# GpSimd tied to VectorE's planned order, no normalisation on GpSimd, re-priced plan and one copy less a pair in an attention and two-expert-layer kernel

## The chip, the cores and the metric

One core of one Trainium2 chip. The time is the device time of one execution in microseconds; the median of three runs counts. The engines are named as in the profile: PE is TensorE (PEld its weight load), DVE is VectorE, ACT is ScalarE, POOL is GpSimd, SP is SyncE, whose queue issues the DMAs.

## The reference

Three layers, all in fp32, for 4 batches of 448 tokens with a model width of 768.

```python
# 1. causal attention: q, k, v are (4, 12, 448, 64)
scores = scale * q @ k.T;  scores = where(above the diagonal, -1e9, scores)
attn = exp(scores - max);  attn = attn / (sum(attn) + 1e-9);  x = attn @ v
# 2. gated convolution layer: w_in (768, 1024), conv_w (3, 1024), w_out (1024, 768)
h = maximum(x @ w_in, 0)
conv = sum over k of conv_w[k] * h shifted by k - 1 tokens
x = (h * sigmoid(conv)) @ w_out
# 3. four experts, each one head of causal attention with its own wq, wk, wv (768, 64) and wo (64, 768)
logits = x @ w_gate;  the two largest of four get softmax weights w
out = sum over experts of w[e] * (attention_e(x) @ wo[e])
```

## The kernel before

Every fp32 operand of a large product is split into a high part and a low part (`high` at L666 copies it rounded, `low` at L677 subtracts the high part), and a product is three matmuls: high x high, low x high, high x low (`products`). The output weights of layer 2 are multiplied once into the projections of layer 3 (`fold`), so the kernel runs, for each batch: attention over 6 pairs of heads, 8 feed-forward parts (`ffn_in`), the projections of the experts (`project`), attention over 2 pairs of experts, and the output product (`output`).

Attention of a pair (`scores`, `norms`, `weigh`): 24 score matmuls into PSUM; DVE adds the mask and takes the extreme (L711); ACT takes the exponential and its sum (L715); each of 10 pieces of the weights `e` is then multiplied by the reciprocal of its sum (`norm` inside `norms`: L760 on ACT, L763 on DVE or GpSimd, of 64, 192, 320 or 384 columns; for experts the gate is multiplied in as well, and then ACT is not allowed); 14 transposes on PE (L781) put the weights into PSUM tiles `ta` and `tb`, 8 copies (L670 on ACT, L672 on DVE) bring them to the SBUF tile `z`, and 16 matmuls (L814) multiply the values. There is one tile `z`. Two of the 8 copies have 512 columns, two 256, and four 128 on 64 partitions. The result is again split into high and low.

No engine's order is written by hand. Each step is an operation of a `Plan` with a price for each engine that may run it (`scale_cost`, `psum_cost`, `copy_cost`, `two_cost`) and lags between engines (`LAG`). The planner runs list scheduling: it picks engine and start of each operation by rank, and the instructions are emitted in order of planned start. The ranks come from backward passes and are then changed by a long list of adjustments, `SHIFTS`; a list entry adds a constant or a noise of a seed to the ranks of some operations. On the chip each engine runs its instructions in the order emitted, and waits only for what it reads and overwrites. In the plan, operations that use the SBUF port shared by DVE and GpSimd (every GpSimd operation, and those of DVE whose `port` has a "V") exclude one another; the emitted program does not hold to that.

Six dummy matmuls (`WARM`) and thirty more (`FILLS`) run on PE ahead of the first data.

Of the kernel before, what the change touches and what calls it, by code (L numbers as in the profile page):

```python
# [17 lines left out]
B, H, S, D = 4, 12, 448, 64  # L18
# [25 lines left out]
KEYS = ((0, 448), (448, 320), (832, 192), (768, 64))  # L44


def spread(z, width, first, step, n):
# [168 lines left out]
class Plan:  # L216
# [4 lines left out]
    LAG = {"TT": 0.0, "TA": 0.2, "TV": 0.2, "TG": 0.27, "TD": 0.19, "AT": 0.23, "AA": 0.0, "AV": 0.16, "AG": 0.17, "AD": 0.14,  # L221
# [130 lines left out]
    def run(self):  # L352
# [35 lines left out]
        if SHIFTS and forward(rank) >= best[0]:  # L388
            forward(best[1])
        for o in sorted(self.ops, key=lambda o: (o.start, o.n)):  # L390
            o.fn(o.engine)

# [149 lines left out]

ON = {"qk high": ("AVG", "AVG"), "qk low": "VG", "gx": "AG", "w high": "AVG", "w low": "VG"}
# [16 lines left out]
def scale_cost(n, on="AVG"):  # L560
    return only(on, {"A": on_scalar(n) + 0.137, "V": on_vector2(n) + 0.065, "G": 0.245 + n * 0.000835})
# [6 lines left out]
def psum_cost(n, on="A"):  # L568
    return dict(only(on, {"A": on_scalar(n), "V": on_vector(n)}))
# [5 lines left out]


@with_exitstack
def attention_moe_moe(ctx: ExitStack, tc: tile.TileContext, qk, vv, w_in, cw, w_out, wqk, wvg, wo, out):
    nc = tc.nc
    ctx.enter_context(tc.manual_schedule())  # L580
    P = Plan()

    w1d = nc.dram_tensor("w1_scratch", (NF, 128, 2 * DM), F32, kind="Internal").ap()
    wod = nc.dram_tensor("wo_scratch", (2, 128, 2 * DM), F32, kind="Internal").ap()

    base = ctx.enter_context(tc.tile_pool(name="base", bufs=1))
    psum = ctx.enter_context(tc.tile_pool(name="psum", bufs=1, space=PSUM))
# [629 lines left out]
```

## Time and profile before

| what | value |
|---|---|
| median of three runs | 534.32 us (533.75 to 536.55) |
| the profiled execution | 535.11 us, span of its instructions 533.3 us |
| granted TensorE clock, mean over the span | 0.992 of full speed |
| busy: PE, DVE, ACT, POOL | 515.4, 421.6, 357.7, 112.0 us |
| DMA | 69.92 MB, 131 GB/s over the span |

The span runs from the first instruction to the end of the last one, and the execution's own time is 1.8 us longer. Busy time of PE counts a matmul from its issue to a modelled end, so matmuls that queue behind each other are counted as busy as well. Times in the trace are from the span's start.

### The profile page before, as it was taken

To read this page: it belongs to the slowest core of one execution; us is meant where nothing else is said; L and a number is where in the kernel's file an instruction comes from. 1 tells how busy PE (TensorE), PEld (TensorE's weight loads), DVE (VectorE), ACT (ScalarE), POOL (GpSimd) and SP (SyncE) were. 2 spreads that over 40 slices of the span, in tenths; PEclk is the share of its full clock that TensorE was granted. 3 is DMA by queue.
4 is the path that set the end of the run, shared out by engine and by line. 5 is a ranking of instruction groups with operands and counts; after the bars stand their busy time and mean duration, and the time that the engine had idled before them with its cause. 6 is when DMAs were issued, how large, how long until landed. Compare 5 with 4: busy or idle time off the path is not lost.

```text
span 533.3 us, 10436 instructions
## 1 busy us (share of the span) xinstructions
PE 515.4 (97%) x3554; PEld 436.2 (82%) x3556; DVE 421.6 (79%) x1300; ACT 357.7 (67%) x1058; POOL 112.0 (21%) x132
## 2 busy tenths in 40 slices
PE   8799999899899999899999999999999999999997
PEld 4678888778689898798898777998987778989875
DVE  6999599889798549999259999986389999842581
ACT  2876279789986557686249986755488867732572
POOL 3152017334232021160012511101114000000010
PEclk9999999899989999999999999999999999999999
DMA  9984246845587011374201573763003315610042
GB/s 239 256 222 135 63 149 195 255 120 206 167 246 201 23 36 37 139 250 163 68 2 46 146 219 84 249 215 87 1 1 113 117 49 194 221 59 1 10 154 104
DMA packets 63381, 69.92 MB, mean 131 GB/s; under 512 B 36576, under 2 KB 57312, under 8 KB 63328
## 3 DMA queue, kind: packets, MB, share of 16 engines
q1 hardware_dynamic: 63328, 69.26, 42.7%
q8 instruction: 28, 0.46, 0.4%
q14 instruction: 25, 0.20, 0.1%
HBM read 55.87 MB, written 13.37 MB: 130 GB/s over the span
## 4 chain that ended last, share of the span: by engine, by line
PE 47%; DVE 25%; ACT 8%; issue 2%; ACTq 0%; DVEq 0%
PE pf L966 34%; DVE e L711 7%; DVE e L763 5%; PE bank L814 5%; DVE z L672 4%; PE bank L781 3%; ACT e L715 3%; PE bank L734 3%; ACT e L760 2%; DVE pair L678 1%; DVE pair L672 1%; DVE work L995 1%; PE bank L966 1%; ACT z L670 1%; PE pf L1074 1%
## 5 line engine op out<-in xcount | busy, mean ns | idle before, releaser
L966 PE MATMUL pf<-pair,slab 128*128 128x448 f32 (+2 forms) x984 | 218.5, 368 | 4.3 <-ACT hp L984 2.7
L966 PEld LDWEIGHTS pf<-pair,slab 128*128 128x128 f32 x984 | 171.8, 189 | 22.2 <-ACT hp L984 3.7
L715 ACT ACTIVATE e<-e,stat 128x192 f32<-128x192 f32 (+3 forms) x256 | 127.1, 499 | 23.8 <-DVE stat L711 23.4
L711 DVE CUSTOM_DVE_ANT_0 e<-bank,mask 128x448 f32<-128x448 f32 (+3 forms) x256 | 92.1, 414 | 6.7 <-PE bank L734 6.5
L966 PE MATMUL pf<-pair,wqks 128*128 128x448 f32 x384 | 81.1, 369 | 0.0
L966 PEld LDWEIGHTS pf<-pair,wqks 128*128 128x128 f32 x384 | 71.4, 188 | 7.0 <-ACT pair L670 0.3
L781 PE MATMUL bank<-ident,e 128*128 128x128 f32 x448 | 70.7, 280 | 6.4 <-DVE stat L711 3.5
L678 POOL TENSOR_TENSOR pair<-work,pair 128x448 fp32r<-128x448 f32 (+1 forms) x39 | 48.6, 1260 | 105.6 <-PE bank L734 39.1
L781 PEld LDWEIGHTS bank<-ident,e 128*128 128x128 f32 x448 | 52.7, 142 | 16.9 <-DVE stat L711 3.6
L672 DVE COPY z<-bank 64x128 f32<-64x128 f32 (+2 forms) x121 | 48.7, 429 | 20.9 <-PE bank L781 16.7
L670 ACT ACTIVATE z<-bank 64x128 f32<-64x128 f32 (+2 forms) x135 | 45.8, 367 | 13.4 <-PE bank L814 7.4
L760 ACT ACTIVATE e<-e,stat 64x64 f32<-64x64 f32 (+3 forms) x116 | 49.4, 454 | 7.5 <-DVE stat L755 5.9
L734 PE MATMUL bank<-pair,pair 64*128 64x448 f32 (+3 forms) x576 | 49.6, 291 | 0.1
L814 PE MATMUL bank<-z,block 128*64 128x448 f32 (+3 forms) x384 | 48.7, 395 | 0.0
L715 ACT ACTIVATION_READ_ACCUMULATOR e<-e,stat 128x1 f32 (+1 forms) x256 | 48.5, 189 | 0.0
L995 DVE SCALAR_TENSOR_TENSOR work<-hp,cws,work 128x448 f32<-128x448 f32 x64 | 43.7, 694 | 3.9 <-ACT work L990 3.3
L734 PEld LDWEIGHTS bank<-pair,pair 64*128 64x128 f32 (+1 forms) x576 | 41.9, 172 | 3.3 <-issue 1.6
L814 PEld LDWEIGHTS bank<-z,block 128*64 128x64 f32 x384 | 27.3, 139 | 20.6 <-issue 11.5
L966 PE MATMUL pf<-wvs,pair 128*128 128x260 f32 x288 | 37.3, 286 | 0.0
L678 DVE TENSOR_TENSOR pair<-pf,pair 64x448 fp32r<-64x448 f32 (+1 forms) x24 | 15.0, 623 | 26.7 <-ACT pair L670 26.4
L966 PEld LDWEIGHTS pf<-wvs,pair 128*128 128x128 f32 x288 | 35.5, 188 | 0.3
L670 ACT ACTIVATE pair<-pf 64x448 fp32r<-64x448 f32 (+1 forms) x24 | 12.8, 541 | 32.3 <-PE pf L966 32.0
(99 smaller groups left out, 593.7 us busy)
## 6 DMA issues: line engine op xcount, KB each, us to landing
slab<-w_scratch SPq DMA_DIRECT2D x24, 768.0 KB, 4.6
work<-in_w_out SPq DMA_DIRECT2D x8, 768.0 KB, 4.8
work<-in_w_in SPq DMA_DIRECT2D x8, 768.0 KB, 5.7
w_scratch<-slab SPq DMA_DIRECT2D x8, 768.0 KB, 4.5
work<-in_qk SPq DMA_DIRECT2D x48, 112.0 KB, 3.4
work<-in_qk SPq DMA_DIRECT2D x24, 224.0 KB, 4.3
out<-work SPq DMA_DIRECT2D x24, 224.0 KB, 2.1
slab<-wo_scratch SPq DMA_DIRECT2D x6, 768.0 KB, 4.3
```

The source lines that it names most:

```text
L670: nc.scalar.activation(dst(), src(), AF.Copy)
L672: nc.vector.tensor_copy(dst(), src())
L678: return lambda e: engine(e).tensor_sub(dst(), src(), f32(h()))
L711: nc.vector.tensor_tensor_reduce(out=ec(o, c), in0=bank(o, c), in1=m, scale=-0.125, scalar=3.0e38, op0=OP.add, op1=OP.min, accum_out=st[ro ...
L715: nc.scalar.activation(ec(o, c), ec(o, c), AF.Exp, bias=st[rows, 0, o, c:c + 1], scale=-1.0, accum_out=st[rows, 1, o, c:c + 1])
L734: nc.tensor.matmul(bank(o, c), q(s)[own, Q0[c]:Q0[c] + QN[c]], k(t)[own, kc(o, c)], start=i == 0, stop=i == 2)
L760: nc.scalar.activation(dst(), src(), AF.Copy, scale=st[rows, 3, o, c:c + 1])
L763: engine(en).tensor_scalar(dst(), src(), st[rows, 3, o, c:c + 1], gate, op0=OP.mult, op1=OP.mult)
L781: P.op({"T": TURN}, lambda _: nc.tensor.transpose(dst(), src(), ident[:, :]), r=r, w=keys)
L814: nc.tensor.matmul(ps[own, S - n:S], v(k, o), z[:, 1024 * o + n0:1024 * o + n0 + n], start=k == 0, stop=k == 3)
L966: nc.tensor.matmul(out_ap(), a(), b(), start=first, stop=end), r=r, w=[(ps, 0)])
L995: return lambda _: nc.vector.scalar_tensor_tensor(cv[:, :S], hp[:, i:S + i], cws[:, fc, i:i + 1], cv[:, :S], op0=OP.mult, op1=OP.add)
```

## The change

- `LAG["AA"]`, between dependent ACT operations, goes from 0.0 to 0.15. `scale_cost` becomes dearer by 0.053 (ACT), 0.05 (DVE) and 0.055 (GpSimd), `psum_cost` by 0.12 below 64 columns and by 0.065 up to 128. The convolution's first step keeps its old price.
- `norm` may run on ACT or DVE (attention) or DVE only (experts); GpSimd is no longer allowed.
- On emission, the first instruction of each GpSimd operation gets a dependency on the last instruction of the port-using DVE operation emitted just before it, if that one was planned to start less than 3 us earlier.
- The columns of `z` are laid out anew (`KEYS`), so that what was copied from `ta` in two copies of 256 columns is copied in one of 512.
- The last output tile is copied and stored in two halves.
- `SHIFTS` is a new list.

```diff
-KEYS = ((0, 448), (448, 320), (832, 192), (768, 64))
+KEYS = ((0, 448), (704, 320), (512, 192), (448, 64))
...
-    LAG = {"TT": 0.0, "TA": 0.2, "TV": 0.2, "TG": 0.27, "TD": 0.19, "AT": 0.23, "AA": 0.0, "AV": 0.16, "AG": 0.17, "AD": 0.14,
+    LAG = {"TT": 0.0, "TA": 0.2, "TV": 0.2, "TG": 0.27, "TD": 0.19, "AT": 0.23, "AA": 0.15, "AV": 0.16, "AG": 0.17, "AD": 0.14,
...
+        body, near = self.nc.cur_bb.bb, None
         for o in sorted(self.ops, key=lambda o: (o.start, o.n)):
+            n = len(body.instructions)
             o.fn(o.engine)
+            new = body.instructions[n:]
+            if o.engine == "V" and "V" in o.port:
+                near = o, new[-1].name
+            elif o.engine == "G" and near and near[0].start > o.start - 3:
+                self.tc.add_manual_dep(new[0], near[1], mybir.DependencyInfo(mybir.DependencyClass.Sync, mybir.DependencyReason.DATA), reason="port")
...
+NORM = ("AV", "V")
...
-    return only(on, {"A": on_scalar(n) + 0.137, "V": on_vector2(n) + 0.065, "G": 0.245 + n * 0.000835})
+    return only(on, {"A": on_scalar(n) + 0.19, "V": on_vector2(n) + 0.115, "G": 0.3 + n * 0.000835})
...
-    return dict(only(on, {"A": on_scalar(n), "V": on_vector(n)}))
+    more = 0.12 if n < 64 else 0.065 if n <= 128 else 0.0
+    return dict(only(on, {"A": on_scalar(n) + more, "V": on_vector(n) + more}))
...
-            P.op(scale_cost(n, "VG" if moe else "AVG"), fn, r=r + [(st, "r")] + ([(COEF, b)] if moe else []), w=w)
+            P.op(scale_cost(n, NORM[moe]), fn, r=r + [(st, "r")] + ([(COEF, b)] if moe else []), w=w)
...
-            for o in range(2):
-                P.op(psum_cost(256, "AV"), high(lambda o=o: spread(z, 2048, 1024 * o + 64, 832, 128),
-                                                lambda t=t, o=o: t[:, 256 * o:256 * o + 256].rearrange("p (b c) -> p b c", b=2)),
-                     r=[(t, 2 * o), (t, 2 * o + 1)], w=[(z, (o, 3))])
+            P.op(psum_cost(512, "AV"), high(lambda: z[:, :].rearrange("p (a b) -> p a b", a=4)[:, :, 64:192],
+                                            lambda t=t: t[:, :].rearrange("p (a b) -> p a b", a=4)), r=[(t, j) for j in range(4)], w=[(z, 3)])
...
-            P.op(scale_cost(S, "A"), c1, r=[(hp, 0), (CWS, 0)], w=[(cv, 0)])
+            P.op({"A": on_scalar(S) + 0.137}, c1, r=[(hp, 0), (CWS, 0)], w=[(cv, 0)])
...
-            P.op(psum_cost(S, "AV"), high(lambda o=o: o[:, :S], lambda ps=ps: ps[:, :S]), r=[(ps, 0)], w=[(o, 0)])
+            parts = 1 + (b + 1 == B and dc + 1 == NK)
+            for i in range(parts):
+                own = slice(i * S // parts, (i + 1) * S // parts)
+                P.op(psum_cost(S // parts, "AV"), high(lambda o=o, own=own: o[:, own], lambda ps=ps, own=own: ps[:, own]), r=[(ps, 0)], w=[(o, i)])
+                P.op(dma_cost(229376 // parts, 1792 // parts), lambda _, dc=dc, o=o, own=own: nc.sync.dma_start(out[b, dc][:, own], o[:, own]), r=[(o, i)])
```

## Rows read from the trace of the kernel before

**Rows 1.** The page's part 1: busy time, share of the span, instructions.

```profile
PE 515.4 (97%) x3554; PEld 436.2 (82%) x3556; DVE 421.6 (79%) x1300; ACT 357.7 (67%) x1058; POOL 112.0 (21%) x132
```

**Rows 2.** The chain that ended last: start, length in us, what.

```profile
153.64 1.70 PE bank L734 x24
...
184.46 1.88 PE bank L814 x16
...
335.69 22.49 PE pf L966 x111
...
388.39 1.31 PE bank L781 x12
...
529.86 0.55 ACT work L670
```

**Rows 3.** By stretch: length, busy of PE, PEld, DVE, ACT, POOL, clock, DMA share, GB/s.

```profile
80.00:145.00 65.00, 60.64 (x433) 50.60 (x429) 57.91 (x161) 58.55 (x173) 29.62 (x31) 0.97 0.63 191
195.00:240.00 45.00, 43.62 (x313) 37.49 (x312) 43.16 (x150) 33.78 (x105) 12.06 (x12) 1.00 0.39 126
275.00:321.00 46.00, 44.85 (x388) 36.08 (x382) 44.16 (x178) 41.83 (x137) 16.44 (x22) 1.00 0.43 121
...
400.00:440.00 40.00, 38.72 (x325) 29.72 (x324) 39.00 (x151) 32.08 (x109) 8.20 (x13) 1.00 0.28 93
```

**Rows 4.** The page's part 4: that chain's shares of the span by engine.

```profile
PE 47%; DVE 25%; ACT 8%; issue 2%; ACTq 0%; DVEq 0%
```

**Rows 5.** L763 alone, whole span: busy of DVE, POOL, clock, DMA share, GB/s.

```profile
0.00:533.30 533.30, 54.22 (x151) 31.19 (x53) 0.99 0.43 131
```

**Rows 6.** L763 on GpSimd: count, duration in ns (least/median/most), first and last start, shapes.

```profile
L763 POOL TENSOR_SCALAR e<-e,stat x42: 313/538/1123, 18.7 to 428.3; 64x64 f32<-64x64 f32 x15, 128x384 f32<-128x384 f32 x12, 128x320 f32<-128x320 f32 x9, 128x192 f32<-128x192 f32 x6
...
L763 POOL TENSOR_SCALAR e<-e,stat,coef x11: 390/606/4227, 211.8 to 511.2; 64x64 f32<-64x64 f32 x4, 128x320 f32<-128x320 f32 x3, 128x192 f32<-128x192 f32 x2, 128x384 f32<-128x384 f32 x2
```

**Rows 7.** DVE by shape in 440:459: busy us, mean ns, idle before.

```profile
L678 DVE TENSOR_TENSOR pair<-work,pair 128x448 fp32r<-128x448 f32 x4 | 2.4, 622 | 0.1
...
L763 DVE TENSOR_SCALAR e<-e,stat,coef 64x64 f32<-64x64 f32 x4 | 1.2, 310 | 0.1
...
L763 DVE TENSOR_SCALAR e<-e,stat,coef 128x384 f32<-128x384 f32 x2 | 0.9, 478 | 0.0
L763 DVE TENSOR_SCALAR e<-e,stat,coef 128x320 f32<-128x320 f32 x2 | 0.8, 434 | 0.0
...
L763 DVE TENSOR_SCALAR e<-e,stat,coef 128x192 f32<-128x192 f32 x2 | 0.7, 379 | 0.0
```

**Rows 8.** ACT by shape, whole span.

```profile
L670 ACT ACTIVATE z<-bank 128x512 f32<-128x512 f32 x30 | 17.3, 588 | 2.2 <-PE bank L781 1.9
...
L760 ACT ACTIVATE e<-e,stat 64x64 f32<-64x64 f32 x48 | 15.9, 344 | 1.0
L760 ACT ACTIVATE e<-e,stat 128x384 f32<-128x384 f32 x21 | 12.8, 609 | 0.1
...
L670 ACT ACTIVATE z<-bank 128x256 f32<-128x256 f32 x34 | 11.7, 379 | 2.6 <-PE bank L781 2.3
```

**Rows 9.** DVE by shape, whole span.

```profile
L678 DVE TENSOR_TENSOR pair<-work,pair 128x448 fp32r<-128x448 f32 x45 | 29.1, 652 | 1.6 <-ACT pair L670 1.2
L672 DVE COPY z<-bank 128x512 f32<-128x512 f32 x34 | 22.8, 683 | 10.1 <-PE bank L781 6.4 <-PE bank L814 3.3
...
L672 DVE COPY z<-bank 128x256 f32<-128x256 f32 x30 | 11.4, 413 | 5.5 <-PE bank L781 5.5
```

**Rows 10.** The timeline around 391.2 us: start, length, engine, instruction.

```profile
391.19 1.16 POOL L678 TENSOR_TENSOR pair<-work,pair 128x448 fp32r<-128x448 f32 x1
391.26 1.28 DVE L763 TENSOR_SCALAR e<-e,stat 128x320 f32<-128x320 f32 x1
```

**Rows 11.** Waits of DVE and of PE: total us, times, longest.

```profile
DVE pair L678 <- ACT pair L670: 31.6, 17, 4.8
...
PE pf L966 <- POOL pair L678: 0.4, 1, 0.4
```

More of the change, by code (lines that the diff above doesn't have):

```diff
@@ L581, in attention_moe_moe @@
     P = Plan()
+    P.tc, P.nc = tc, nc
     w1d = nc.dram_tensor("w1_scratch", (NF, 128, 2 * DM), F32, kind="Internal").ap()
@@ L791, in weigh @@
         for o, own in enumerate(HALF):
-            P.op(psum_cost(128, "AV"), high(lambda own=own, o=o: spread(z, 2048, 1024 * o, 448, 64)[own],
+            P.op(psum_cost(128, "AV"), high(lambda own=own, o=o: spread(z, 2048, 1024 * o, 704, 64)[own],
                                             lambda own=own, t=t: t[own, :128].rearrange("p (b c) -> p b c", b=2)), r=[(t, 1)], w=[(z, (o, 0))])
-            P.op(psum_cost(128, "AV"), high(lambda own=own, o=o: z[own, 1024 * o + 768:1024 * o + 896], lambda own=own, t=t: t[own, 128:256]),
+            P.op(psum_cost(128, "AV"), high(lambda own=own, o=o: z[own, 1024 * o + 448:1024 * o + 576], lambda own=own, t=t: t[own, 128:256]),
                  r=[(t, 2)], w=[(z, (o, 1))])
@@ L802, in weigh @@
             if i < 2:
-                P.op(psum_cost(512, "AV"), high(lambda i=i: spread(z, 2048, 1024 * i + 192, 320, 256), lambda t=t: t[:, :].rearrange("p (b c) -> p b c", b=2)),
+                P.op(psum_cost(512, "AV"), high(lambda i=i: spread(z, 2048, 1024 * i + 192, 576, 256), lambda t=t: t[:, :].rearrange("p (b c) -> p b c", b=2)),
                      r=[(t, j) for j in range(4)], w=[(z, (i, 2))])
                 continue
-            for o in range(2):
-                P.op(psum_cost(256, "AV"), high(lambda o=o: spread(z, 2048, 1024 * o + 64, 832, 128),
-                                                lambda t=t, o=o: t[:, 256 * o:256 * o + 256].rearrange("p (b c) -> p b c", b=2)),
-                     r=[(t, 2 * o), (t, 2 * o + 1)], w=[(z, (o, 3))])
+            P.op(psum_cost(512, "AV"), high(lambda: z[:, :].rearrange("p (a b) -> p a b", a=4)[:, :, 64:192],
+                                            lambda t=t: t[:, :].rearrange("p (a b) -> p a b", a=4)), r=[(t, j) for j in range(4)], w=[(z, 3)])
         def rest(_):
@@ L814, in rest @@
                     nc.tensor.matmul(ps[own, S - n:S], v(k, o), z[:, 1024 * o + n0:1024 * o + n0 + n], start=k == 0, stop=k == 3)
-        P.op({"T": 4 * 960 / 2400 + 0.23}, rest, r=[(z, (o, i)) for o in range(2) for i in range(4)] + v_r, w=[(ps, 0)], mode=2)
+        P.op({"T": 4 * 960 / 2400 + 0.23}, rest, r=[(z, (o, i)) for o in range(2) for i in range(3)] + [(z, 3)] + v_r, w=[(ps, 0)], mode=2)
         P.op(psum_cost(S, "AV"), high(lambda: dst[:, 0], lambda: ps[:, :S]), r=[(ps, 0)], w=[(dst, 0)])
@@ L1153, in output @@
                  [(hi, 0)], [(lo, 0)], [(ys[p], 0)], [(ys[p], 1)]) for p in range(2)])
-            P.op(psum_cost(S, "AV"), high(lambda o=o: o[:, :S], lambda ps=ps: ps[:, :S]), r=[(ps, 0)], w=[(o, 0)])
-            P.op(dma_cost(229376, 1792), lambda _, dc=dc, o=o: nc.sync.dma_start(out[b, dc], o[:, :S]), r=[(o, 0)])
+            parts = 1 + (b + 1 == B and dc + 1 == NK)
[3 more added lines that the diff above has]
+                P.op(dma_cost(229376 // parts, 1792 // parts), lambda _, dc=dc, o=o, own=own: nc.sync.dma_start(out[b, dc][:, own], o[:, own]), r=[(o, i)])
     xs = attention(0)
```

120 rows, old and new, of the table SHIFTS are left out of this document.

## The prediction, made before the change was run

> **What bounds the kernel now.** I read the busy times of the engines first [rows 1]. TensorE is marked busy for 515.4 of 533.3 us, but a matmul that waits in the pipeline counts as busy, so I price its work by itself. Stretches of the chain of waits in which TensorE runs without a stop [rows 2] give: 22.49 us for 111 matmuls of 448 columns, 0.2026 us each; 1.31 us for 12 transposes, 0.109 us; 1.70 us for the 24 score matmuls of a pair of heads; 1.88 us for its 16 value matmuls. From the loops of the code there are 1104 products of 448 columns, 144 of 512, 496 of 260, 496 transposes and 32 pairs. With the other widths priced by columns the work is 1104 x 0.2026 + 144 x 0.2316 + 496 x 0.1176 + 496 x 0.109 + 32 x 3.58 = 223.7 + 33.3 + 58.3 + 54.1 + 114.6 = 484 us. So 49 us of the span are not TensorE work. The tail behind the last matmul takes 3.4 (the last ACT copy begins at 529.86), the 36 dummy matmuls ahead of the first data some 8 (36 x 0.2316). About 37 us are left, lost in the middle.
>
> The table of busy time by stretch says where [rows 3]. In 195:240, 275:321 and 400:440 VectorE (DVE) is busy 43.16 of 45, 44.16 of 46 and 39.00 of 40 us: these stretches, with 80:145 where ACT is as full as DVE, carry most of the attention work. Over the whole span DVE is busy only 79% [rows 1], so elsewhere it has room while TensorE runs dense. The summary of the chain [rows 4] agrees: a quarter of the span hangs on DVE work, 8% on ACT. So the time is TensorE's work plus what the crowded DVE stretches cost it, and an edit is worth what it takes from DVE there, or what the order moves out of there.
>
> **The change part by part.**
>
> *No normalisation on GpSimd.* 53 instructions leave it, 31.19 us of its time [rows 5]. Their shapes [rows 6]: in the attention stages 15 of 64 columns, 9 of 320, 12 of 384, 6 of 192; in the expert stages (they multiply by a gate) 4, 3, 2, 2. Prices on DVE come from a stretch with hardly any GpSimd work [rows 7]: 0.310, 0.434, 0.478, 0.379. The 11 expert ones can go to DVE only: 4 x 0.310 + 3 x 0.434 + 2 x 0.478 + 2 x 0.379 = 4.3 us. The 42 others would cost DVE 16.6, or ACT 20.2 (0.344 and 0.609 for 64 and 384 columns [rows 8], 0.45 and 0.56 between them for 192 and 320). I take them halved between the engines: DVE +8.3, ACT +10.1. Bounds: DVE +4.3 to +20.9 altogether. ACT has 6.4 + 11.2 + 4.2 + 7.9 = 30 us free in the four crowded stretches [rows 3], which hides its share; without that cover it would cost up to 10.
>
> *One copy less a pair.* The new layout of z lets one 512-column copy replace two of 256. ACT: 2 x 0.379 - 0.588 = 0.170 us saved [rows 8]; DVE: 2 x 0.413 - 0.683 = 0.143 [rows 9]. Over 32 pairs, half on each: DVE -2.3, ACT -2.7. The Trainium skill (Perfetto Trace Analysis, "Optimizing Scalar/DVE Operations") puts the fixed part of a PSUM access at about 125 ns on DVE and 51 ns on ACT; by it the saving is an estimated -2.0 and -0.8, so the trace is kinder to ACT, and DVE's term would move by 0.3 us. The other side: the copy now waits for all four transposes, and the last one to land takes 0.59 to 0.68 instead of 0.38 to 0.41, so z is whole 0.21 to 0.27 us later for each pair, 6.7 to 8.6 us over 32 if bare. I cost it at nothing: between the transposes and the value matmuls TensorE has products of the feed-forward part to run, and in crowded stretches DVE's total counts, not one pair's latency.
>
> *GpSimd waits for the DVE instruction planned just ahead of it.* What it is to cure is in one pair of rows [rows 10]: a GpSimd subtraction of 1.16 us starts 0.07 us before a DVE normalisation of 320 columns, and that takes 1.28 us instead of 0.434: it ends when GpSimd ends. The sum of this is less than the one case looks. The 45 DVE subtractions between SBUF tiles average 0.652 [rows 9] against 0.622 undisturbed [rows 7]: 0.03 each, 1.35 us. With some 290 such instructions (the 45 subtractions, 151 normalisations [rows 5], 64 and up to 32 of the convolution) at that rate it is 8.8 us. Between 1.35 and 8.8 I take 6, as longer single cases exist; two thirds go away: DVE -4. Bounds: 0 to -8.8. For the cost of the wait: behind a waiting GpSimd instruction stand the next low halves of its queue, and for these waits TensorE. It waited for GpSimd's halves once in the whole profile, 0.4 us [rows 11], and GpSimd's 112.0 us [rows 1] fall by 31, so I cost the wait at nothing; were each of the 79 remaining GpSimd instructions late by one DVE instruction (0.62 us), 49 us of GpSimd idleness would still fit in its 533.
>
> *Freed GpSimd time.* 31.19 us hold 26 subtractions of 1.16 us. Each taken from DVE saves 0.622. The planner chooses the engine; I count half, 13: DVE -8.1 (bounds 0 and -16).
>
> *Split last output.* The last copy of 448 columns (0.55 us on ACT [rows 2]) becomes two of 224, one on each engine, each with its own store. Half of the copy goes: -0.3 us. Bounds: 0 (the second store is queued behind the first on SP) to -0.55.
>
> *Measured prices and new order.* The planner's price of an ACT normalisation of 384 columns was 0.05 + 0.32 + 0.137 = 0.507 against 0.609 in the row; now it is 0.56. For 64 columns it was 0.240 against 0.344. For an ACT instruction that feeds another it now adds 0.15. So plan and execution drift apart less, and with engines that run in order, drift is what makes one late instruction hold up everything behind it. The ranks that set the order are a wholly new list. What this is worth no row shows. Above: the 37 us lost in the middle. Below: an order can open a new wait, and the longest of the DVE waits for ACT's high half was 4.8 us [rows 11]: +4.8. Most of the DVE work stays and TensorE stays near its 484, so I stay far from the upper end: a fifth, -7.
>
> *Sum.* DVE in the crowded stretches: +4.3 + 8.3 - 2.3 - 4 - 8.1 = -1.8. Last output -0.3, order -7: -9.1. On the profiled execution's 535.1 that is 526.0; this execution lies 0.8 above the median of 534.3, so 525.2.
>
> **Rivals.**
>
> *A larger gain from the order.* If half of the 37 us comes back, as the higher GpSimd share and the closer prices allow: -18 - 2 = -20, 514. For it: DVE is idle for 21% of the span [rows 1] while it is full in the crowded stretches [rows 3]. Against: the batches depend on each other, so attention can be moved only so far.
>
> *No change.* DVE ends even (the planner moves no subtractions: +6.3) and the order gives back just that: 533, anywhere in 531.6 to 537.0, which is 0.5%, about what a measurement of this kernel can tell from no change.
>
> *Slower: the collisions change sides.* The added wait is one-sided: GpSimd waits for DVE, DVE never for GpSimd. A GpSimd instruction now starts just when the DVE one ahead of it ends, which is when DVE begins its next; if that one also works between SBUF tiles, DVE stands for the whole of it, as in [rows 10]. The place is the crowded stretches. Price: 35 subtractions there now (48 for queries and keys and 32 for the gate values, less DVE's 45) plus 13 more, 48, each holding DVE for half of 1.16 us in half of the cases (the other half read PSUM) is 48 x 0.58 x 0.5 = +14; without the -4 and without an order gain DVE has +2.2 + 14, 550; with half of these prices 542. It decides when more than a third of the GpSimd instructions are followed on DVE by an instruction between SBUF tiles. For it: nothing on DVE's side waits. Against: the planner itself keeps such instructions apart, and DVE has PSUM readers to put beside them. The Trainium skill (SBUF — State Buffer, "Who interferes with whom") states this as a rule: whoever of the two issues first has the shared pair for its whole instruction and the other blocks. By that rule the trace agrees in the 1.28 us row, and by it the wait alone moves a stall and does not remove it.
>
> **How the numbers follow.** Forecast case, 519 to 531.6: 0.50. Larger gain, below 519: 0.17. No change: 0.19. Slower: 0.14. Faster is 0.50 + 0.17 = 0.67. The time is that of the likeliest, 525.2. The range takes the larger gain down to 512 and the no-change case up to 537 and leaves out the slower one and a little below: 512 to 537. The forecast case alone is 519 to 531.6.
>
> **What would show it.** Right: no normalisation left on GpSimd; mean time of DVE subtractions between SBUF tiles near 0.62 and of the cast and normalisation forms near their undisturbed values; 32 more 512-column copies and no 256-column ones; more than 35 subtractions on GpSimd; less DVE-bound chain than a quarter of the span; the last matmul some 9 us earlier. Wrong: GpSimd rows that end DVE's idle or stretch its instructions more than now, TensorE waiting for GpSimd's low halves, or DVE full over longer stretches than the four. The prediction fails most easily in the size of the order's term, which is a choice within wide bounds.

## The result and the profile after

The changed kernel takes 522.04 us (median of 4 runs, 521.72 to 522.63) against 534.15 (median of 4): ratio 0.9758, 95% interval 0.9732 to 0.9784, 12.1 us faster. The prediction was 525.2, within 512 to 537. The profiled execution took 521.82 us, its span 520.0.

The page of the changed kernel, parts 1 and 4, answers [rows 1] and [rows 4]:

```profile
PE 510.4 (98%) x3556; PEld 434.5 (84%) x3556; DVE 416.7 (80%) x1313; ACT 357.4 (69%) x1062; POOL 79.3 (15%) x86
...
PE 86%; DVE 8%; ACT 3%; DMA 1%; issue 1%; SPq 0%; ACTq 0%
```

GpSimd's work falls by 32.7 us and DVE's falls too, by 4.9, although DVE now does more normalisations. The chain that ended last runs through DVE for 8% of the span where it was 25%. It is one path through a crowd of near-equal ones, so this is a sign and not a sum of time.

By stretch (the columns are those of [rows 3]):

```profile
80.00:150.00 70.00, 69.87 (x523) 57.30 (x520) 68.48 (x200) 62.23 (x186) 16.67 (x14) 1.00 0.72 222
...
260.00:360.00 100.00, 99.57 (x753) 84.84 (x753) 91.86 (x324) 84.61 (x263) 20.82 (x22) 1.00 0.46 133
...
390.00:440.00 50.00, 49.78 (x383) 40.90 (x380) 48.18 (x182) 41.86 (x134) 5.32 (x7) 1.00 0.34 112
```

The crowded stretches are still there, with DVE at 68.48 of 70 and 48.18 of 50 us. But TensorE is hardly ever empty in them: 69.87 of 70, where before it was 60.64 of 65 in 80:145.

L789 (L763 before) alone on DVE, the whole span, against [rows 5]:

```profile
0.00:520.00 520.00, 60.17 (x191) 1.00 0.45 134
```

So 40 of the 53 normalisations went to DVE, which has 191 instead of 151, and 13 to ACT; DVE's time in them grew by 6.0 us only. The shapes on DVE (against [rows 7] and [rows 9]; a shape without `coef` is the plain normalisation, one with it also multiplies by a gate):

```profile
L704 DVE TENSOR_TENSOR pair<-work,pair 128x448 fp32r<-128x448 f32 x49 | 29.5, 617 | 0.9 <-ACT pair L696 0.6
L698 DVE COPY z<-bank 128x512 f32<-128x512 f32 x34 | 22.8, 684 | 12.5 <-PE bank L807 7.8 <-PE bank L838 4.5
...
L789 DVE TENSOR_SCALAR e<-e,stat 128x384 f32<-128x384 f32 x28 | 11.4, 411 | 0.1
...
L789 DVE TENSOR_SCALAR e<-e,stat 64x64 f32<-64x64 f32 x41 | 9.8, 255 | 1.0 <-ACT e L786 0.3
L789 DVE TENSOR_SCALAR e<-e,stat,coef 64x64 f32<-64x64 f32 x32 | 9.6, 309 | 0.5
...
L789 DVE TENSOR_SCALAR e<-e,stat 128x320 f32<-128x320 f32 x23 | 8.5, 388 | 0.2
L789 DVE TENSOR_SCALAR e<-e,stat,coef 128x384 f32<-128x384 f32 x16 | 7.3, 474 | 0.2
...
L789 DVE TENSOR_SCALAR e<-e,stat 128x192 f32<-128x192 f32 x19 | 5.6, 314 | 0.2
```

The plain normalisations of the kernel before:

```profile
L763 DVE TENSOR_SCALAR e<-e,stat 64x64 f32<-64x64 f32 x33 | 9.9, 306 | 1.0 <-ACT e L760 0.4
...
L763 DVE TENSOR_SCALAR e<-e,stat 128x320 f32<-128x320 f32 x18 | 8.6, 487 | 0.3
L763 DVE TENSOR_SCALAR e<-e,stat 128x384 f32<-128x384 f32 x15 | 6.7, 454 | 0.2
...
L763 DVE TENSOR_SCALAR e<-e,stat 128x192 f32<-128x192 f32 x16 | 6.0, 381 | 0.2
```

Subtractions between SBUF tiles take 617 ns instead of 652, the plain normalisations of 64, 192, 320 and 384 columns 255, 314, 388 and 411 instead of 306, 381, 487 and 454. The wait, the order and the engines all changed between these two profiles, so the means alone do not say which of them did it. DVE has 49 subtractions, not fewer than the 45 of before, so GpSimd was not given more of them: its 35 became 31, by the groups on GpSimd.

```profile
L704 POOL TENSOR_TENSOR pair<-work,pair 128x448 fp32r<-128x448 f32 x31 | 35.3, 1157 | 74.5 <-PE bank L807 24.0 <-DVE work L913 20.8 <-DVE e L789 20.1
```

By the groups on ACT and on DVE the z copies of 512 columns are 62 and 34, and none of 256 is left; the row of ACT:

```profile
L696 ACT ACTIVATE z<-bank 128x512 f32<-128x512 f32 x62 | 35.3, 595 | 5.0 <-PE bank L807 4.0
```

The end, in the timeline:

```profile
516.61 0.60 ACT L696 ACTIVATE work<-bank 128x224 f32<-128x224 f32 x2 [0.47 <-PE bank L990]
```

Both halves of the last output were planned on ACT, 0.60 us together against 0.55 for the whole one before, and the span ends 3.4 us after they begin, as before.

### The profile page after: what moved, and what is told of

It is laid out like the page before. It is cut to its first block, busy times and chain, and to the rows that moved or that the text cites. A ratio compares the mean times of both kernels' runs of the same rounds, so it can differ in the third digit from the quotient of the medians.

```text
span 520.0 us, 10393 instructions
## 1 busy us (share of the span) xinstructions
PE 510.4 (98%) x3556; PEld 434.5 (84%) x3556; DVE 416.7 (80%) x1313; ACT 357.4 (69%) x1062; POOL 79.3 (15%) x86
## 4 chain that ended last, share of the span: by engine, by line
PE 86%; DVE 8%; ACT 3%; DMA 1%; issue 1%; SPq 0%; ACTq 0%
PE pf L990 56%; PE bank L838 9%; PE bank L807 9%; PE bank L760 8%; DVE e L737 3%; PE pf L1187 2%; DVE e L789 2%; DMA work<-in_wqk 1%; ACT e L741 1%; PE pf L1098 1%; DVE z L698 1%; PE bank L990 1%; ACT e L786 1%; DVE pair L704 1%; PE pf L675 1%
## 5 line engine op out<-in xcount | busy, mean ns | idle before, releaser
L741 ACT ACTIVATE e<-e,stat 128x320 f32<-128x320 f32 (+3 forms) x256 | 127.1, 500 | 17.7 <-DVE stat L737 17.4
L737 DVE CUSTOM_DVE_ANT_0 e<-bank,mask 64x64 f32<-64x64 f32 (+3 forms) x256 | 93.1, 413 | 16.4 <-PE bank L760 15.6
L696 ACT ACTIVATE z<-bank 128x512 f32<-128x512 f32 (+1 forms) x133 | 53.2, 421 | 15.2 <-PE bank L838 8.5
L704 POOL TENSOR_TENSOR pair<-work,pair 128x448 fp32r<-128x448 f32 (+1 forms) x35 | 42.6, 1236 | 87.4 <-DVE work L913 33.6
L786 ACT ACTIVATE e<-e,stat 64x64 f32<-64x64 f32 (+3 forms) x129 | 52.0, 448 | 4.6 <-DVE stat L781 3.6
L698 DVE COPY z<-bank 64x128 f32<-64x128 f32 (+1 forms) x91 | 38.0, 434 | 20.9 <-PE bank L807 11.9
L838 PE MATMUL bank<-z,block 128*64 128x448 f32 (+3 forms) x384 | 46.9, 386 | 0.0
L990 PE MATMUL pf<-wvs,pair 128*128 128x260 f32 x288 | 39.6, 288 | 0.0
L700 POOL TENSOR_SCALAR pair<-work 128x896 fp32r<-128x896 f32 (+2 forms) x17 | 15.2, 895 | 145.4 <-DMA block<-in_vv 43.7
```

The lines of the kernel that those rows point to most:

```text
L696: nc.scalar.activation(dst(), src(), AF.Copy)
L698: nc.vector.tensor_copy(dst(), src())
L700: nc.gpsimd.tensor_scalar(dst(), src(), 1.0, 1.0, op0=OP.mult, op1=OP.mult)
L704: return lambda e: engine(e).tensor_sub(dst(), src(), f32(h()))
L737: nc.vector.tensor_tensor_reduce(out=ec(o, c), in0=bank(o, c), in1=m, scale=-0.125, scalar=3.0e38, op0=OP.add, op1=OP.min, accum_out=st[ro ...
L741: nc.scalar.activation(ec(o, c), ec(o, c), AF.Exp, bias=st[rows, 0, o, c:c + 1], scale=-1.0, accum_out=st[rows, 1, o, c:c + 1])
```

## The experiments

Each run was compared with the kernel before on the same chip; its median there was 533.3 for the first four runs, 533.6 for the next four and 533.9 for the last four. The ratios are those on record; they differ by up to 0.2% from the quotient of the medians given here. "Order" means which engine runs each operation and in which sequence.

**1. The changed kernel without the wait.**

```diff
             elif o.engine == "G" and near and near[0].start > o.start - 3:
-                self.tc.add_manual_dep(new[0], near[1], mybir.DependencyInfo(mybir.DependencyClass.Sync, mybir.DependencyReason.DATA), reason="port")
+                pass
```

> The changed kernel, its order and engines kept, without the added dependencies of GpSimd on DVE. If the wait carries the gain: GpSimd starts early again, DVE subtractions between SBUF tiles go from 617 back to 652 ns and the plain normalisations of 320 columns from 388 towards 487, DVE gets 5 to 9 us longer, time 526 to 531. If the order and the planner's choice of engines carry it: at most 2 us are lost, 521.5 to 524.

531.01 us, ratio 0.9946 (0.9917 to 0.9975): 9.0 us slower than with the wait, three quarters of the whole gain. Its page, two shapes on DVE and one on GpSimd:

```profile
PE 513.7 (97%) x3555; PEld 436.1 (82%) x3556; DVE 425.5 (80%) x1313; ACT 357.6 (68%) x1062; POOL 86.3 (16%) x86
...
L789 DVE TENSOR_SCALAR e<-e,stat 128x384 f32<-128x384 f32 x28 | 13.6, 490 | 0.1
...
L789 DVE TENSOR_SCALAR e<-e,stat 128x192 f32<-128x192 f32 x19 | 8.4, 459 | 0.2
...
L704 POOL TENSOR_TENSOR pair<-work,pair 128x448 fp32r<-128x448 f32 x31 | 38.8, 1269 | 74.9 <-PE pf L1098 30.5 <-PE bank L807 21.1 <-DVE pair L698 15.9
```

With the same instructions in the same order, DVE is busy 8.8 us longer (425.5 against 416.7) and GpSimd 7.0 (86.3 against 79.3): a collision stretches either side. The time and DVE's total came as expected, the shapes did not: normalisations of 320 columns went to 401 ns only (487 expected) and subtractions to 640; the loss sits in 192 columns (314 to 459) and 384 (411 to 490). One collision in its timeline:

```profile
313.38 1.32 POOL L704 TENSOR_TENSOR pair<-work,pair 128x448 fp32r<-128x448 f32 x1
313.62 1.30 DVE L789 TENSOR_SCALAR e<-e,stat 128x384 f32<-128x384 f32 x1
```

A normalisation of 384 columns on DVE, 0.411 us in the changed kernel, begins 0.24 us after a subtraction on GpSimd, takes 1.30 us and ends 0.22 us behind it. The Trainium skill (SBUF — State Buffer, "Who interferes with whom") says that the one that issues second blocks for the whole instruction of the other; the trace agrees in this pair, and on GpSimd the mean subtraction grows from 1157 to 1269 ns.

**2. The kernel before with the wait alone.** The same lines added to the old kernel, whose order stays.

> The kernel before in its own order with only the dependencies of GpSimd on DVE added. If the collisions cost what I took them for: DVE 4 to 9 us shorter, 525 to 531. If the order carries the gain: 532 to 536. If the collisions only change sides or GpSimd's results come late: 538 or more.

526.66 us, ratio 0.986 (0.9833 to 0.9887): 6.6 us faster. The page:

```profile
PE 511.7 (97%) x3554; PEld 434.3 (83%) x3556; DVE 413.6 (79%) x1300; ACT 356.9 (68%) x1058; POOL 104.2 (20%) x132
```

DVE is 8.0 us shorter than in [rows 1] and GpSimd 7.8, with nothing else changed. The normalisations alone (busy on DVE and GpSimd, against [rows 5]), then by shape on DVE:

```profile
0.00:526.00 526.00, 48.83 (x151) 25.85 (x53) 1.00 0.44 133
...
L687 DVE TENSOR_TENSOR pair<-work,pair 128x448 fp32r<-128x448 f32 x45 | 29.3, 657 | 1.5 <-ACT pair L679 1.0
...
L772 DVE TENSOR_SCALAR e<-e,stat 64x64 f32<-64x64 f32 x33 | 8.0, 247 | 0.6
...
L772 DVE TENSOR_SCALAR e<-e,stat 128x320 f32<-128x320 f32 x18 | 7.6, 429 | 0.3
```

The normalisations fall (306 to 247 ns, 487 to 429), all 151 of them together from 54.22 us to 48.83. The subtractions, from which the prediction took its price, do not (652 to 657). So in both orders the wait carries the larger part of the gain, and the prediction, which put 7 us on prices and order and 4 on the wait, had the weights the wrong way round.

**3. The copies.** The merged copy's operation emits two of 256 columns on the same engine, and the order stays.

```diff
-            P.op(psum_cost(512, "AV"), high(lambda: z[:, :].rearrange("p (a b) -> p a b", a=4)[:, :, 64:192],
-                                            lambda t=t: t[:, :].rearrange("p (a b) -> p a b", a=4)), r=[(t, j) for j in range(4)], w=[(z, 3)])
+            def two(e, t=t):
+                for o in range(2):
+                    high(lambda: z[:, 1024 * o:1024 * o + 1024].rearrange("p (a b) -> p a b", a=2)[:, :, 64:192],
+                         lambda: t[:, 256 * o:256 * o + 256].rearrange("p (a b) -> p a b", a=2))(e)
+
+            P.op(psum_cost(512, "AV"), two, r=[(t, j) for j in range(4)], w=[(z, 3)])
```

> The changed kernel in its order, but each merged copy of 512 columns is emitted as two of 256 on the same engine. By the rows of before that is 0.170 us more on ACT and 0.143 on DVE each time, 32 times, 5 us over both engines. If engine time in the crowded stretches counts: 523.5 to 526. If the copy is hidden beside TensorE: 521.5 to 523.

521.98 us, ratio 0.9779 (0.9753 to 0.9804): no difference from 522.04. By the counts, 27 of the merged copies ran on ACT and 5 on DVE. ACT's busy time was 358.7 against 357.4 and DVE's 417.3 against 416.7, 1.9 us in all where the rows had promised 5. One reason is in the row of the halves:

```profile
L696 ACT ACTIVATE z<-bank 128x256 f32<-128x256 f32 x54 | 17.7, 382 | 4.4 <-PE bank L807 3.9
```

54 copies of 382 ns would be 20.6 us, but they occupy 17.7: one begins before the other has ended, and a difference of mean durations counts this overlap as work. What is left of the price is hidden in this order.

**4. Normalisations moved without a new plan.** The kernel before, the 53 normalisations of GpSimd emitted on DVE at the same place.

```diff
             def fn(en):
+                en = "V" if en == "G" else en
```

> The kernel before in its own order, but the 53 normalisations planned for GpSimd run on DVE at the same place in the order. If DVE's time in the crowded stretches sets the end: 53 x about 0.39 us, 20.8 us more on DVE less some 5 us of collisions, time 540 to 550. If normalisations on GpSimd cost DVE by collisions as much as they relieve it: 531 to 537.

546.18 us, ratio 1.0232 (1.0209 to 1.0255), 12.9 us slower. DVE is busy 433.2 us, 11.6 more than before, where 53 times 0.39 would be 20.8. The time follows DVE's, as it would if DVE set the end, and the move alone, without the wait, cost as much as the change gained. All its executions also ran at a mean clock of 0.99, which is worth some 2 us in the kernel before (last section). With a plan made for it, keeping normalisations off GpSimd cost 3.4 and 0.6 us (runs 5 and 6).

**5. Orders without a search.** Four kernels with `SHIFTS` empty, so that the planner's own ranks stand: the changed kernel; the kernel before with the wait; the changed kernel with old prices (`"AA": 0.0`, the old `scale_cost`, `more = 0.0`); the changed kernel with `NORM = ("AVG", "VG")`.

> The changed kernel with an empty list of adjustments, so that the order is that of the planner's own ranks; everything else, the wait too, is kept. If the list is worth what the order's term of -7 meant and more: 529 to 540. If the order hardly counts once GpSimd waits: 521 to 525.

> The kernel before with the wait of GpSimd on DVE and an empty list: to be held against the changed kernel with an empty list, which has the new prices, the one copy less and no normalisation on GpSimd. If these edits of the plan help by themselves: 4 us or more slower than that kernel. If what the changed kernel has beyond the wait is its searched order: within 3 us of it, or faster.

> The changed kernel with an empty list and the old prices (the lag between ACT operations 0, normalisations and small copies at the old cost). If prices nearer to the trace make the better order: 2 to 6 us slower than with the new prices. If prices of this size only shuffle the order: within 3 us on either side.

> The changed kernel with an empty list, normalisations allowed on GpSimd again. If GpSimd relieves DVE and ACT also when it waits: 2 to 6 us faster than without. If a normalisation on GpSimd costs more by its wait and by holding the port than it relieves: the same or up to 5 us slower.

Medians and ratios to before, in that order: 534.14 us (1.0001, 0.9976 to 1.0026), 540.87 (1.0125, 1.0103 to 1.0147), 541.25 (1.0125, 1.0104 to 1.0146), 530.72 (0.9933, 0.9912 to 0.9953). The list is worth 12.1 us to the changed kernel (534.14 - 522.04) and 14.2 to the old one with the wait (540.87 - 526.66), so a better list is not what separates the two. The lists were not exchanged: their entries name operations by number and by planned time, which differ. Without lists the changed plan is 6.7 us better than the old one, and the prices, taken alone, make 7.1.

**6. Is that chance of the order?** The same with one entry that adds a noise to all ranks, applied whatever its plan is.

```diff
-SHIFTS = ()
+SHIFTS = ((1, 0, 600, 0.5),)
...
-        if SHIFTS and forward(rank) >= best[0]:
-            forward(best[1])
+        forward(rank)
```

> The changed kernel with the list replaced by one entry that adds a noise of 0.5 to all ranks, the same one in the two runs that follow. It tells how far an unsearched order moves the time by chance: near 534.1 (within 3 us) if the differences seen with the empty list can be trusted, further off if they are chance of the order.

> The same noise with the old prices. If the prices are worth what they were with the empty list: 5 to 9 us slower than the shuffled order with the new prices. If that difference was chance of the order: within 3 us of it or faster.

> The same noise with normalisations allowed on GpSimd. If GpSimd relieves the others there as with the empty list: 2 to 5 us faster than the shuffled order without them. If that difference was chance: within 2 us, or slower.

540.66 us (ratio 1.0124, 1.0095 to 1.0152), 547.62 (1.0266, 1.0225 to 1.0307) and 540.04 (1.0109, 1.0074 to 1.0143). The noise itself costs 6.5 us, twice what was expected of an order by chance, so a single unsearched order says little. The old prices lose 7.0 again, after 7.1, but two differences of the size of that chance suggest a gain and do not show it. Normalisations on GpSimd gain 0.6 after 3.4, within what an order does by chance. How the prices help is not seen: the old ones gave DVE 11.1 us more work with the empty list (432.9 against 421.8 busy), but 0.7 more with the noise (427.3 against 426.6).

**7. The rule on both sides.** A port-using DVE operation also waits for the GpSimd operation emitted before it.

```diff
             if o.engine == "V" and "V" in o.port:
                 near = o, new[-1].name
+                if last and last[0].start > o.start - 3:
+                    self.tc.add_manual_dep(new[0], last[1], mybir.DependencyInfo(mybir.DependencyClass.Sync, mybir.DependencyReason.DATA), reason="port")
...
+                last = o, new[-1].name
```

> The changed kernel in its order, with the rule made two-sided: a port-using DVE operation also waits for the GpSimd operation emitted just before it. If DVE only stands where the port would have held it anyway: 521 to 523.5. If GpSimd often runs later than planned, DVE now waits where it went first until now: 524 to 530, and DVE's largest waits are for GpSimd.

524.48 us, ratio 0.9822 (0.979 to 0.9853), 2.4 slower than the changed kernel. DVE is busy 2.0 us less (414.7), but it now stands for GpSimd; its largest wait, and the first two of twelve for GpSimd (us in total, times, longest):

```profile
DVE pair L708 <- ACT pair L700: 27.3, 11, 5.3
...
DVE work L1031 <- POOL gx L704: 1.0, 2, 0.5
...
DVE cws L913 <- POOL pair L708: 0.8, 1, 0.8
```

Together the twelve are 5.9 us. The time is in the range expected for a DVE that now waits where it went first until now, but, against the expectation, its largest waits are still those for ACT. The one-sided wait is the better one, and no version tried beats the changed kernel by more than noise.

## Why the prediction was right, and which of its terms were not

The sign and the range held, and so did the mechanism that DVE time in the crowded stretches is what counts: where only the wait differs, 8.0 and 8.8 us of DVE went with 6.6 and 9.0 us of time. Most terms were off, in both directions, so the closeness of the sum is partly luck.

*The wait*, taken at -4 with a bound of -8.8: this term was mis-sized. Runs 2 and 1 put it at -6.6 and -9.0 us of time and -8.0 and -8.8 of DVE. I read 0.03 us from the subtractions and carried it over to all forms. But run 2 leaves the subtractions at 657 ns and shortens the plain normalisations, for which I had no undisturbed row, by 28 to 60. That the bound, 290 times 0.03, is near the measured values is luck. In [rows 10] the normalisation ends 0.19 us behind GpSimd's instruction and not with it. Costing the wait on GpSimd at nothing was right: TensorE's waits in the changed kernel name no GpSimd instruction, in run 2 they name one, of 0.2 us.

*No normalisation on GpSimd*, taken at +12.6 on DVE by halves, which is 32 more on DVE at 0.39 us. It became 40, and against run 2, which has the wait as well, they cost 60.17 - 48.83 = 11.3 us, 0.28 each: more of them at a lower price, so the sum is near by luck. Part of the low price is that run 2 still has collisions (429 ns for 320 columns against 388). My price was wrong in kind: [rows 7] has the forms that multiply by a gate, 474 ns for 384 columns here against 411 for the plain form.

*Freed GpSimd time*, -8.1: did not happen, GpSimd subtracts 31 times and not 48. GpSimd just idles more.

*The copy*, -2.3 on DVE and -2.7 on ACT: 0 in the time, and 0.6 and 1.3 us of busy time (run 3). The subtraction of mean durations overstated it, and for ACT the -0.8 that stands beside it in the prediction is the nearer one. No cost of waiting for four transposes shows either. *The split output*, -0.3: nothing, as both halves went to ACT.

*Prices and order*, -7: mis-sized as well. All that the changed kernel has beyond the wait is 4.6 us when the wait is added first (526.66 - 522.04) and 2.3 when it is added last (533.3 - 531.01). The prediction had -5.1 for the same parts (12.6 - 2.3 - 8.1 - 0.3 - 7). That this is near is luck, as the -8.1, the -2.3 and the -0.3 did not come. The runs with unsearched orders give the prices about 7, twice; against the normalisations on GpSimd they show no gain, the list is worth about the same to both kernels, and the copy nothing. How these pieces make 2 to 5 us in the searched order is not shown; the prices are the one piece with a gain in two orders.

The rival that the collisions change sides was wrong: with the wait DVE's busy time fell in both orders. Why a GpSimd instruction that starts just behind a DVE one so seldom blocks the next was not tried; that the planner keeps port users apart is a likely reason, not a shown one.

## What to carry to other kernels

Where a plan assumes that two engines do not use a shared resource together, the emitted program must hold to it: a dependency on the engine with slack took 6.6 and 9.0 us off two orders here, with no wait of note behind it, while making the crowded engine wait as well cost 2.4. The size of collisions is not to be carried over from one form of instruction to the others; compare each form's mean with a quiet stretch of the same form. The order is worth more than most edits: taking the lists away cost 12 and 14 us and a noise 6.5, so single edits of a planned kernel are compared with the order held fixed, or over several orders.

## What the runs showed of the chip that was not expected

TensorE's clock took part. In the kernel before, by stretch:

```profile
99.00:102.05 3.05, 1.44 (x21) 1.09 (x20) 2.99 (x7) 2.10 (x7) 1.62 (x2) 1.00 1.06 303
102.05:105.46 3.41, 3.41 (x13) 3.09 (x14) 2.77 (x10) 2.41 (x8) 1.39 (x2) 0.50 1.05 313
143.00:146.42 3.42, 1.60 (x11) 1.22 (x12) 2.14 (x4) 3.39 (x8) 0.00 (x0) 1.00 0.69 225
146.42:149.84 3.42, 3.42 (x17) 2.39 (x14) 3.36 (x7) 2.89 (x8) 0.00 (x0) 0.50 0.73 258
```

Twice, after stretches in which TensorE was busy 1.44 of 3.05 us and 1.60 of 3.42 us, the granted clock was 0.50 (1.2 GHz) for 3.4 us and then 1.00 (2.4 GHz) again. At half the rate 3.4 us do 1.7 us of work, so by estimate the two cost up to 3.4. The first of these gaps has a collision ahead of it, seen in the same trace:

```profile
97.48 3.22 DVE L763 TENSOR_SCALAR e<-e,stat 128x192 f32<-128x192 f32 x6
...
97.74 2.05 POOL L678 TENSOR_TENSOR slab<-work,slab 128x768 fp32r<-128x768 f32 x1 [0.29 <-ACT slab L670]
...
101.95 1.49 PE L781 MATMUL bank<-ident,e 128*128 128x128 f32 x6 [1.57 <-DVE pair L678]
```

Six normalisations (the row names the shape of the first; they have 64 to 384 columns) take 3.22 us beside a GpSimd subtraction of 2.05, the work queued behind them on DVE is late, and TensorE stands 1.57 us for it. The second gap ended with a wait for ACT. The changed kernel without the wait has such stretches as well, one of them here:

```profile
130.50:133.94 3.44, 3.44 (x12) 2.82 (x12) 3.44 (x17) 2.89 (x9) 0.17 (x1) 0.50 0.91 249
```

The profiles of the kernel before with the wait and of the changed kernel show a mean clock of 1.000. But the clock is the smaller part. Not every execution of the kernel before has such stretches: of the 28 measured beside runs 1 to 7, the 14 with a mean clock of at least 0.999 have a median of 532.91 us and the 9 below 0.995 one of 535.15. At a mean clock of at least 0.999 on both sides, the wait is still worth 6.2 us in the old order (532.91 to 526.66, four executions) and 8.1 in the new one (529.89 to 521.82, three each). By these few executions less than 1 us of the 6.6 and of the 9.0 goes with the clock.

A normalisation that takes a second scalar per partition is dearer on DVE than the plain one: 309 against 255 ns for 64 columns, 474 against 411 for 384.
